# A gather moved, a third block's rows transposed inside its arm, and the last expert's block in two copies

## The chip, the core and the metric

The kernel runs on one core of one Trainium2 chip. The metric is the time of one execution on the device in microseconds (us). The program is timed in several executions, and the median counts.

The core has five engines, each with its own instruction queue: TensorE (PE, with its weight loads as PEld), VectorE (DVE), ScalarE (ACT), GpSimd (POOL) and SyncE (SP, which here issues most DMA transfers). They meet through semaphores.

## What is computed

Three layers one after the other: windowed attention, a soft mixture of experts, and a mixture in which each token goes to one expert or to none. The change touches the last one alone:

```python
def _moe2_ref(x, w_skip, w_gate, w1, w2):
    N, D = x.shape                      # 1152 tokens, 512
    E = w_gate.shape[1]                 # 8 experts, hidden width 1024
    do_compute = x @ w_skip > 0
    out = x.copy()
    xc = x[do_compute]
    logits = xc @ w_gate
    e_idx = np.argmax(logits, axis=1)
    logits_s = logits - logits.max(-1, keepdims=True)
    probs = np.exp(logits_s)
    probs /= probs.sum(-1, keepdims=True) + 1e-09
    gate_w = probs[np.arange(len(xc)), e_idx]
    y = np.zeros_like(xc)
    for e in range(E):
        mask = e_idx == e
        h = np.maximum(xc[mask] @ w1[e], 0.0)
        y[mask] = gate_w[mask, None] * (h @ w2[e])
    out[do_compute] = xc + y
    return out
```

With the inputs that are timed, experts 0 to 7 get 116, 207, 129, 66, 298, 17, 114 and 51 tokens.

## The kernel before

**Arithmetic.** All matrix products run on TensorE in a 32-bit format on operands that are split into a high and a low part; the products high x high, high x low and low x high are added up in PSUM. So weights and rows each pass a split: ACT copies the high part (L347 for weights, L896 for rows, `xs`), VectorE subtracts it from the original (L351, L898). The tiles of weights are `wa1h`, `wa1l`, `wa2h`, `wa2l` and the same with `wb`: two sets that the experts use in turn, the digit for the first or second layer.

**Blocks.** The last stage, from about 486 us on, handles each expert's tokens in blocks of 128 rows. POOL gathers a block's rows from memory with an indirect DMA (`gather`, L869, into `xg`, or `xj` for a third block), by indices that the routing has computed (`idg`). `xpose` turns them on TensorE in four transposes of 128x128 (`tr4`, L379), and `xsplit` makes high and low parts. `block(e, j, ...)` is the two layers for block `j` of expert `e`: matmuls at L920, ACT at L944 and L965, VectorE at L968, and at the end VectorE scales by the gate and adds (L1004). POOL's `scatter` (L877) writes the rows to the output. A block with at most 64 rows has a small form in which the high and low parts of 64 rows share one pass of 128 columns.

**Branches.** The first block of each expert always runs (for expert 7, in one of the two forms). What an expert has beyond 128 tokens runs inside `tails(e)`, a branch at L1126: `more` runs the second block in one of two arms, full or small (`rows`, L1081), and a third block inside another branch (L1116). For experts 6 and 7 there is one `tails(6)`, placed ahead of expert 7's first block: inside it lie the tails of both and `deep()`, which serves experts with more than 384 tokens and loads weights again. It is entered if any of these has work (`nv[2] > 0`). Here experts 1, 2 and 4 enter the branch (2 for one row), 4 also its third block, with 42 rows; for experts 0, 3, 5 and for 6 with 7 the branch is jumped. `hint(e)` announces the branch's outcome on PE, ACT, DVE and POOL some way ahead of it, not on SP.

**Order.** The program is written by a planner: `add(engine, cost, function, rd, wr, new, prio)` registers an operation, and `plan.run()` issues all that is registered, engine by engine, by list scheduling with the costs and priorities given. Each engine then works through its queue in that order. Expert 0's block is in one plan with the two layers ahead of it. In it the routing's tables are still being made for the second half of their columns: VectorE's `wy` (L755) feeds the `tab` matmuls on TensorE (L760), from which `gates` and `ids` are worked out, which the end of the block needs.

Of the kernel before, what the change touches and what calls it, by code (L numbers as in the profile page):

```python
# [13 lines left out]
ALU = mybir.AluOpType  # L14
# [9 lines left out]
E2 = 8  # L24
TT = NT // 128
XP, XE, XF = -0.5, 0, 2
# [9 lines left out]
def f32(ap):  # L36
    return ap.bitcast(F32)
# [70 lines left out]
class Plan:  # L108
# [6 lines left out]
    def add(self, eng, dur, fn, rd=(), wr=(), prio=0.0, new=None, slack=0.0):  # L115

        o = Op()
        o.slack = slack
        o.eng, o.dur, o.fn, o.prio, o.seq, o.acq = eng, dur, fn, prio, len(self.ops), list(new or ())
        wr = list(wr) + o.acq  # L120
        deps = set()
        for x in rd:
            if x in self.w:
                deps.add(self.w[x])
        for x in wr:
            if x in self.w:
# [96 lines left out]
def fused_kernel(ctx: ExitStack, tc: tile.TileContext, q, k, v, dp, w1, w2, wskip, wgate, m1, m2, out):  # L223
    nc = tc.nc
    PE, ACT, DVE, POOL, SP = nc.tensor, nc.scalar, nc.vector, nc.gpsimd, nc.sync
# [19 lines left out]
    ident = const.tile([128, 128], F32, name="ident")  # L245
# [36 lines left out]
    add = plan.add  # L282
# [600 lines left out]
    def xpose(b, pr, after=[]):  # L883
        p = pt_r.buf()
        add("PE", 0.44, lambda: tr4(p.tile, b.tile), rd=[b, "ident"] + after, new=[p], prio=pr)
        return xsplit([p], pr)

    def xsplit(ps, pr):

        x, w = M["xs"].buf(), KC // len(ps)  # L890
        for i, p in enumerate(ps):
            ks = range(i * w, (i + 1) * w)
            v = lambda p=p: (p.tile if p.ring is pt_r else p.tile.rearrange("p (a n) -> p a n", a=4))[:, 0:w]
            hi = lambda i=i: x[:, i * w:(i + 1) * w, :, 0]
            lo = lambda i=i: x[:, i * w:(i + 1) * w, :, 1]
            add("ACT", c_act(128 * w), lambda v=v, hi=hi: ACT.copy(out=hi(), in_=v()), rd=[p, "M"] + ([x] if i else []),  # L896
                wr=[(x, "h", k) for k in ks], new=None if i else [x], prio=pr)
            add("DVE", c_dve(128 * w), lambda v=v, hi=hi, lo=lo: DVE.tensor_tensor(out=lo(), in0=v(), in1=f32(hi()), op=ALU.subtract),  # L898
                rd=[p, x] + [(x, "h", k) for k in ks], wr=[(x, "l", k) for k in ks], prio=pr)
            p.close()  # L900
        return x
# [123 lines left out]
    with tc.manual_schedule():  # L1025
# [33 lines left out]
        add("X", 0.0, open_moe2, rd=["pf"], wr=["M"] + [("x2", t) for t in range(TT)] + [(x, f) for x in ("hh", "hl") for f in range(FC)], slack=-0.43)  # L1059
        xgs, xts = {}, {}  # L1060
        for j in range(2):
            xgs[0, j] = gather(0, j, 0.0 if j else 2.0)
        w_pass("r", 1, 1)
        w_pass("r", 1, 2)
        xts[0, 0] = xsplit(first, -5)
# [7 lines left out]
        def over(e, i):  # L1073

            return (nv[0] & (7 * 8 ** e)) > (i - 1) * 8 ** e

        def rows(e, j, x, xt):

            state = ([(b, b.left, b.closed, b.slot) for b in (x, xt)],
                     [(r, len(r.free), None if r.slots is None else list(r.slots)) for r in Ring.made])  # L1080
            with tc.If(over(e, 2 * j + 1), preferred_fallthrough_block=False if e == E2 - 1 and j == 0 else None) as c:  # L1081
                block(e, j, x, xt)
                if j == 0:
                    ahead(e)
                scatter(e, j, x)
                plan.run()
            with c.Else():
                for b, left, closed, slot in state[0]:
                    b.left, b.closed, b.slot = left, closed, slot
                for r, n, slots in state[1]:  # L1090
                    r.free, r.slots = [0.0] * n, slots
                block(e, j, x, xt, small=True)
                if j == 0:
                    ahead(e)
                scatter(e, j, x, 64)
                plan.run()

        def further(e):

            return nv[2] > 0 if e == E2 - 2 else over(e, 2)  # L1100

        def hint(e):

# [10 lines left out]
        def more(e, xt):  # L1114
            for j in (1, 2):
                with tc.If(over(e, 4)) if j == 2 else ExitStack():  # L1116
                    if j == 2 and e >= E2 - 2:
                        xgs[e, j] = gather(e, j)
                    if j == 2 or xt is None:
                        xt = xpose(xgs[e, j], 0)  # L1120
                        plan.run()
                    rows(e, j, xgs[e, j], xt)

        def tails(e, xt):

            with tc.If(further(e), label=f"more{e}", preferred_fallthrough_block=True):  # L1126
                if e < E2 - 2:
                    more(e, xt)
                else:
                    with tc.If(over(e, 2)):  # L1130
                        more(e, xt)
                    with tc.If(over(e + 1, 2)):
                        more(e + 1, None)
                    with tc.If(nv[1] > 0):
                        deep()

        def deep():

            for e in range(E2):
                n = nc.values_load(R["cnt"][0:1, e:e + 1], min_val=0, max_val=NT,  # L1140
                                   skip_runtime_bounds_check_because="counts of at most all tokens")
                with tc.If(n > 384):
                    w_pass("r", e, 1)
                    w_pass("r", e, 2)
                    plan.run()
                    with ExitStack() as levels:
                        for j in range(3, TT):
                            if j > 3:
                                levels.enter_context(tc.If(n > 128 * j))
                            x = gather(e, j)  # L1150
                            block(e, j, x, xpose(x, 0))
                            scatter(e, j, x)
                            plan.run()
            w_pass("r", E2 - 1, 1)
            w_pass("r", E2 - 1, 2)
            plan.run()

        for e in range(E2):
            last = e == E2 - 1
            if e < E2 - 2:  # L1160
                xgs[e, 2] = gather(e, 2, 7, [("g2", 0)])
            if last:
                plan.run()
                rows(e, 0, xgs[e, 0], xts[e, 0])
                continue
            block(e, 0, xgs[e, 0], xts[e, 0], amid=None if e else route_gates)
            if e == 0:
                add("X", 0.0, counts, rd=["cnt"], wr=["nv"], slack=1.5)
            ahead(e)
            xts[e, 1] = xpose(xgs[e, 1], XP, [("g2", XE if e else 3)])  # L1170
            xts[e, 1].pin = e == E2 - 2
            if e:
                w_pass("r", e + 1, 1)
                w_pass("r", e + 1, 2)
            for d in range(1 if e == 0 else 2, 3):
                for j in range(2):
                    if e + d < E2:
                        xgs[e + d, j] = gather(e + d, j, 0 if e else 2 * d + j - 1 + (d == 1 and j), [("g10", 0)] if e else [])
            xts[e + 1, 0] = xpose(xgs[e + 1, 0], XP, [("g2", XF if e else 3)])
            scatter(e, 0, xgs[e, 0])  # L1180
            plan.run(**(OFF if e else dict(SP=1.75, PE=1.4, ACT=2.1, POOL=0.6, DVE=0.6)))
            if e == 0:
                route_ps.close()
                M["mmx"].pool = ctx.enter_context(tc.tile_pool(name="ps_x", bufs=3, space=PSUM))
            tails(e, xts[e, 1])


# [26 lines left out]
```

## Time and profile before

| | us |
|---|---|
| runs shown | 655.6, 651.71, 649.83; median 651.71 |
| the profiled execution | 652.86 |
| its span, first to last instruction | 651.1 |
| PE busy | 627.8 (96%) |
| DVE busy | 315.3 (48%) |
| ACT busy | 234.2 (36%) |
| POOL busy | 70.8 (11%) |

Times in the rows are microseconds from the start of the span. A row of the timeline is one instruction, or several alike in a row (x4): start, duration, engine, line, operation, tiles, shapes; in brackets stands how long the engine had been idle before and what ended that. Matmuls overlap each other, so their spacing says more than the duration. Queue names with a q (POOLq, DVEq) are the instructions of an engine's sequencer: branches, semaphores, drains. The granted clock (PEclk) of a stretch is a share of TensorE's full speed, 2.4 GHz; its other level is 1.2 GHz.

### The profile page before, as it was taken

The numbers are of one execution on the slowest core, as the hardware profiler recorded it, in microseconds if no ns is written. First come the engines' busy times: TensorE is split into PE (matmuls) and PEld (weight loads), VectorE is DVE, ScalarE is ACT, GpSimd is POOL, SyncE is SP. The second block draws the span as 40 slices with busy tenths as digits, with TensorE's granted clock in tenths as the row PEclk, the third lists the DMA queues.
The fourth block names the chain that finished last, engine by engine and source line by source line (L and its number), as shares of the span: only waits on it lengthen the run. The fifth ranks groups of instructions, "written<-read, shape, count | busy, mean of one in ns | idle before, by whom it ended". The sixth has DMA issues, their size and how long they took to land. (4 is left out here: it accounts for less than half of the span.)

```text
span 651.1 us, 9941 instructions
## 1 busy us (share of the span) xinstructions
PE 627.8 (96%) x3794; PEld 550.1 (85%) x3794; DVE 315.3 (48%) x685; ACT 234.2 (36%) x488; POOL 70.8 (11%) x103
## 2 busy tenths in 40 slices
PE   8899999999999999999999999999998999999976
PEld 6688898898989898989898998989896878787865
DVE  5897631127412124512124425436478855871871
ACT  5678630025301013401113311202524644853751
POOL 4123320000000000000000000000004321420310
PEclk9999999999999999999999999999998999999998
DMA  9992100006500004400002502010547967791630
GB/s 225 214 294 65 34 2 1 1 1 209 179 1 1 1 1 129 130 1 0 1 1 97 163 15 82 2 66 32 173 164 281 312 227 260 213 385 62 209 127 9
DMA packets 55688, 71.13 MB, mean 109 GB/s; under 512 B 32921, under 2 KB 32921, under 8 KB 55616
## 3 DMA queue, kind: packets, MB, share of 16 engines
q1 hardware_dynamic: 52912, 62.17, 30.4%
q0 software_dynamic: 2704, 8.02, 4.0%
q8 instruction: 42, 0.69, 0.4%
q14 instruction: 30, 0.25, 0.1%
HBM read 63.48 MB, written 7.47 MB: 109 GB/s over the span
## 5 line engine op out<-in xcount | busy, mean ns | idle before, releaser
L540 PE MATMUL mm<-xth,wa1h 128*128 128x384 f32 (+1 forms) x416 | 137.1, 330 | 0.0
L540 PE MATMUL mm<-xtl,wa1h 128*128 128x384 f32 (+1 forms) x416 | 135.3, 325 | 0.2 <-DVE xtl L489 0.2
L540 PE MATMUL mm<-xth,wa1l 128*128 128x384 f32 (+1 forms) x416 | 135.2, 325 | 0.0
L546 ACT ACTIVATE hh<-mm 128x384 fp32r<-128x384 f32 (+1 forms) x104 | 48.4, 466 | 234.7 <-PE mm L540 229.7
L561 PE MATMUL mm<-wa2h,hh 128*128 128x512 f32 (+1 forms) x296 | 117.0, 395 | 0.0
L548 DVE SCALAR_TENSOR_TENSOR hl<-mm,hh 128x384 fp32r<-128x384 f32 (+1 forms) x104 | 54.6, 526 | 126.2 <-ACT hh L546 125.7
L561 PE MATMUL mm<-wa2h,hl 128*128 128x512 f32 (+1 forms) x296 | 115.1, 389 | 0.0
L561 PE MATMUL mm<-wa2l,hh 128*128 128x512 f32 (+1 forms) x296 | 115.0, 389 | 0.0
L540 PEld LDWEIGHTS mm<-xth,wa1h 128*128 128x128 f32 x416 | 78.3, 188 | 0.7 <-issue 0.2
L540 PEld LDWEIGHTS mm<-xtl,wa1h 128*128 128x128 f32 x416 | 78.3, 188 | 0.8 <-DVE xtl L489 0.4
L540 PEld LDWEIGHTS mm<-xth,wa1l 128*128 128x128 f32 x416 | 78.3, 188 | 0.0
L561 PEld LDWEIGHTS mm<-wa2h,hl 128*128 128x128 f32 x296 | 55.7, 188 | 12.4
L561 PEld LDWEIGHTS mm<-wa2h,hh 128*128 128x128 f32 x296 | 55.8, 188 | 11.2
L561 PEld LDWEIGHTS mm<-wa2l,hh 128*128 128x128 f32 x296 | 55.9, 189 | 11.0
L573 DVE SCALAR_TENSOR_TENSOR x<-mm,prob,x 128x512 f32<-128x512 f32 (+1 forms) x28 | 20.5, 732 | 92.0 <-PE mm L561 91.2
L347 ACT CAST wa2h<-raw 128x1024 fp32r<-128x1024 f32 x32 | 33.4, 1050 | 25.6 <-PE mm L561 18.6
L351 DVE TENSOR_TENSOR wa2l<-raw,wa2h 128x1024 fp32r<-128x1024 f32 x32 | 39.0, 1229 | 5.5 <-ACT wa2h L347 5.5
L784 POOL DMA_INDIRECT x<-scr,id x1 | 1.3, 1254 | 364.5 <-DVE id L801 364.5
L351 DVE TENSOR_TENSOR wa1l<-raw,wa1h 128x1024 fp32r<-128x1024 f32 x32 | 38.1, 1224 | 2.4 <-ACT wa1h L347 2.4
L347 ACT CAST wa1h<-raw 128x1024 fp32r<-128x1024 f32 x32 | 32.0, 1048 | 17.9 <-DMA raw<-in_moe_w_dram 9.7
L968 DVE SCALAR_TENSOR_TENSOR ht<-pt,ht 128x512 fp32r<-128x512 f32 (+2 forms) x27 | 15.1, 568 | 33.1 <-ACT ht L965 30.8
L877 POOL DMA_INDIRECT out_dram<-xg,ids x11 | 16.0, 1458 | 83.1 <-DVE xg L1004 64.4
(202 smaller groups left out, 881.4 us busy)
## 6 DMA issues: line engine op xcount, KB each, us to landing
raw<-in_moe_w_dram SPq DMA_DIRECT2D x96, 512.0 KB
scr<-x SPq DMA_DIRECT2D x9, 256.0 KB
out_dram<-x SPq DMA_DIRECT2D x9, 256.0 KB
qn<-in_q_dram SPq DMA_DIRECT2D x8, 256.0 KB
kn<-in_k_dram SPq DMA_DIRECT2D x8, 256.0 KB
vn<-in_v_dram SPq DMA_DIRECT2D x8, 256.0 KB
qn<-in_q_dram SPq DMA_DIRECT2D x2, 128.0 KB
kn<-in_k_dram SPq DMA_DIRECT2D x2, 128.0 KB
```

The costliest lines, as they stand in the source:

```text
L347: (POOL.tensor_copy if hpool else DVE.tensor_copy if hdve else ACT.copy)(out=aps()[0], in_=b.tile)
L351: (POOL if pool else DVE).tensor_tensor(out=l, in0=b.tile, in1=f32(h), op=ALU.subtract)
L540: PE.matmul(out=ps[:, 0:n], lhsT=wa[a][:, kk, f * 128:(f + 1) * 128], rhs=x[:, kk, g0:g0 + n], start=(i == 0), stop=(i == 3 * KC - 1))
L546: add("ACT", c_act(n), lambda: ACT.activation(out=hh[:, f, 0:n], in_=ps[:, 0:n], func=ACTF.Relu), rd=[ps], wr=[("hh", f)], prio=-1)
L548: add("DVE", c_dve(n), lambda: DVE.scalar_tensor_tensor(out=hl[:, f, 0:n], in0=ps[:, 0:n], scalar=0.0, in1=f32(hh[:, f, 0:n]), op0=ALU.max ...
L561: PE.matmul(out=ps[:, 0:c1 - c0], lhsT=x[:, f, o:o + 128], rhs=wa[a][:, f, c0:c1], start=(f == 0 and i == 0), stop=(f == FC - 1 and i == 2))
L573: DVE.scalar_tensor_tensor(out=z, in0=y, scalar=prob[:, t, e:e + 1], in1=z, op0=ALU.mult, op1=ALU.add)
L784: add("POOL", 1.0, lambda: POOL.indirect_dma_start(out=R["x0"], out_offset=None, in_=scr[0:128 * (GT + 1), :], in_offset=bass.IndirectOffs ...
L877: add("POOL", 1.0, lambda: POOL.indirect_dma_start(out=out, out_offset=bass.IndirectOffsetOnAxis(ap=R["ids"][0:n, j, e:e + 1], axis=0), in ...
L968: add("DVE", c_dve(w * n), lambda: DVE.scalar_tensor_tensor(out=ht[:, s, n:2 * n], in0=p[:, 0:w, 0:n], scalar=0.0, in1=f32(ht[:, s, 0:n]), ...
```

## The change

1. **Expert 0.** `xts[0, 1]`, the transposed rows of its second block, is no longer made ahead of `tails(0)`; it is made inside the arm if that runs. The gather (0, 1) gets priority 2.5 in place of 0.0, and so goes behind (1, 0) and (0, 0).
2. **Blocks that were not transposed ahead**, third blocks above all, are transposed inside their arm by `xpair`, in two pieces of two transposes each, over 128 rows in the full arm and 64 in the small one, in place of one `xpose` of 128 rows ahead of the branch on the block's size. `xsplit` gets a width `n` for that.
3. **Experts 6 and 7.** `tails(6)` is gone. `last()` tests `nv[2] == 0`: if so, expert 7's block runs (`rows`, first copy); in the other arm come the tails of 6 and 7, `deep()`, and `rows` a second time. The hint is turned round with it. `keep` and `back` save and restore the planner's state of buffers between the two copies.

```diff
+    def xpair(b, n):
+        ps = [pt_r.buf() for _ in range(2)]
+        for i, p in enumerate(ps):
+            def tr(i=i, p=p):
+                for g in range(2):
+                    PE.transpose(out=p[:, g, 0:n], in_=b[0:n, 256 * i + 128 * g:256 * i + 128 * g + 128],
+                                 identity=ident[0:n, 0:n])
+
+            add("PE", 0.22, tr, rd=[b, "ident"], new=[p], prio=0)
+        return xsplit(ps, 0, n)
+
-    def xsplit(ps, pr):
+    def xsplit(ps, pr, n=128):
...
-            xgs[0, j] = gather(0, j, 0.0 if j else 2.0)
+            xgs[0, j] = gather(0, j, 2.5 if j else 2.0)
...
-                block(e, j, x, xt)
+                block(e, j, x, xt or xpair(x, 128))
...
-                block(e, j, x, xt, small=True)
+                block(e, j, x, xt or xpair(x, 64), small=True)
...
-            return nv[2] > 0 if e == E2 - 2 else over(e, 2)
+            return nv[2] == 0 if e == E2 - 2 else over(e, 2)
...
-                    if j == 2 or xt is None:
-                        xt = xpose(xgs[e, j], 0)
                         plan.run()
-                    rows(e, j, xgs[e, j], xt)
+                    rows(e, j, xgs[e, j], xt if j == 1 else None)
...
             with tc.If(further(e), label=f"more{e}", preferred_fallthrough_block=True):
-                if e < E2 - 2:
-                    more(e, xt)
-                else:
-                    with tc.If(over(e, 2)):
-                        more(e, xt)
-                    with tc.If(over(e + 1, 2)):
-                        more(e + 1, None)
-                    with tc.If(nv[1] > 0):
-                        deep()
+                more(e, xt)
+
+        def last(xt):
+
+            e = E2 - 1
+            mine = e, 0, xgs[e, 0], xts[e, 0]
+            state = keep(*mine[2:])
+            with tc.If(nv[2] == 0, label=f"more{e - 1}", preferred_fallthrough_block=True) as c:
+                rows(*mine)
+            with c.Else():
+                back(state)
+                with tc.If(over(e - 1, 2)):
+                    more(e - 1, xt)
+                with tc.If(over(e, 2)):
+                    more(e, None)
+                with tc.If(nv[1] > 0):
+                    deep()
+                rows(*mine)
...
-                rows(e, 0, xgs[e, 0], xts[e, 0])
+                last(xts[e - 1, 1])
...
-            xts[e, 1] = xpose(xgs[e, 1], XP, [("g2", XE if e else 3)])
-            xts[e, 1].pin = e == E2 - 2
+            if e:
+                xts[e, 1] = xpose(xgs[e, 1], XP, [("g2", XE)])
+                xts[e, 1].pin = e == E2 - 2
...
-            tails(e, xts[e, 1])
+            if e < E2 - 2:
+                tails(e, xts.get((e, 1)))
```

## Rows read from the trace of the kernel before

**Rows 1.** The page, busy us (share of the span) and instructions of each engine
```profile
PE 627.8 (96%) x3794; PEld 550.1 (85%) x3794; DVE 315.3 (48%) x685; ACT 234.2 (36%) x488; POOL 70.8 (11%) x103
```

**Rows 2.** Windows: length, busy PE, PEld, DVE, ACT, POOL; PEclk, DMA share, GB/s
```profile
505.00:531.00 26.00, 25.03 (x120) 20.30 (x119) 16.93 (x20) 14.28 (x20) 6.55 (x6) 1.00 0.82 285
```

**Rows 3.** Timeline, expert 0's first block
```profile
497.08 0.60 PE L379 MATMUL pt<-ident,xg 128*128 128x128 f32 x4
...
498.72 0.67 DVE L755 TENSOR_TENSOR wy<-w,oj 128x216 bf16<-128x216 bf16 x2
...
500.03 0.73 PE L379 MATMUL pt<-ident,xg 128*128 128x128 f32 x4 [2.35 <-DMA xg<-scr,idg]
...
500.80 0.78 PE L920 MATMUL mm<-wb2h,ht 128*128 128x512 f32 x1
...
504.44 0.48 PE L920 MATMUL mm<-wa1h,xs 128*128 128x512 f32 x1 [0.15 <-PEq L1126]
```

**Rows 4.** Windows around three stops of TensorE
```profile
500.00:504.50 4.50, 4.32 (x15) 3.27 (x15) 4.06 (x10) 0.65 (x1) 1.12 (x1) 0.62 1.02 384
592.00:594.40 2.40, 0.88 (x7) 0.56 (x5) 1.44 (x2) 0.61 (x1) 0.92 (x1) 1.00 0.00 0
...
634.00:637.00 3.00, 3.00 (x7) 2.42 (x8) 0.00 (x0) 0.00 (x0) 0.00 (x0) 0.51 0.08 27
```

**Rows 5.** Timeline, last eight matmuls of expert 3's block and what follows
```profile
564.78 0.40 PE L920 MATMUL mm<-wa2h,ht 128*128 128x512 f32 x1
...
566.97 0.49 PE L920 MATMUL mm<-wb1h,xs 128*128 128x512 f32 x1
```

**Rows 6.** Timeline, expert 4's third block
```profile
592.45 0.75 DVE L1004 SCALAR_TENSOR_TENSOR xg<-mmx,gates,xg 128x512 f32<-128x512 f32 x1 [3.27 <-PE mmx L920]
592.88 0.61 ACT L896 CAST xs<-pt 128x512 fp32r<-128x512 f32 x1 [4.42 <-PE pt L379]
...
593.53 0.69 DVE L898 TENSOR_TENSOR xs<-pt,xs 128x512 fp32r<-128x512 f32 x1 [0.33 <-ACT xs L896]
...
594.36 0.47 PE L920 MATMUL mmx<-wb1h,xs 128*128 128x512 f32 x1 [1.52 <-DVE xs L898]
...
596.30 0.28 PE L920 MATMUL mmx<-wb1h,xs 128*128 128x256 f32 x1
...
601.14 0.28 ACT L965 ACTIVATE ht<-pt 128x128 fp32r<-128x128 f32 x1 [0.87 <-PE pt L959]
...
601.45 0.29 DVE L968 SCALAR_TENSOR_TENSOR ht<-pt,ht 128x128 fp32r<-128x128 f32 x1 [2.01 <-ACT ht L965]
```

**Rows 7.** Timeline, the start of expert 7's block
```profile
630.84 0.47 PE L920 MATMUL mm<-wa1h,xs 128*128 128x512 f32 x1 [0.68 <-PEq L1126]
...
633.99 0.80 PE L920 MATMUL mm<-wa1l,xs 128*128 128x512 f32 x1 [2.67 <-DVEq L1126]
...
637.07 0.28 PE L920 MATMUL mm<-wa1h,xs 128*128 128x256 f32 x1
```

**Rows 8.** Line L1126, 617 to 636: count, ns min/median/max, first and last start
```profile
L1126 SPq EVENT_SEMAPHORE  x9: 17/17/17, 624.4 to 625.7; - x9
...
L1126 DVEq EVENT_SEMAPHORE  x3: 21/21/21, 618.8 to 634.0; - x3
...
L1126 POOLq INC_SWDGE_SEM  x2: 829/841/853, 618.0 to 634.8; - x2
...
L1126 SPq COMPARE_BRANCH  x1: 45/45/45, 619.3 to 619.3; - x1
...
L1126 DVEq COMPARE_BRANCH  x1: 74/74/74, 630.2 to 630.2; - x1
```

**Rows 9.** The end: timeline, then line L1209 on POOL and SP
```profile
646.19 0.91 POOL L877 DMA_INDIRECT out_dram<-xg,ids  x1 [13.22 <-DVE xg L1004]
...
L1209 POOLq DRAIN  x3: 44/115/4094, 646.1 to 650.8; - x3
...
L1209 SPq EVENT_SEMAPHORE  x13: 17/28/13112, 635.6 to 651.0; - x13
```

More of the change, by code (lines that the diff above doesn't have):

```diff
@@ L892, in xsplit @@
             ks = range(i * w, (i + 1) * w)
[L893 to L896, printed above, removed]
+            v = lambda p=p: (p.tile if p.ring is pt_r else p.tile.rearrange("p (a n) -> p a n", a=4))[:, 0:w, 0:n]
+            hi = lambda i=i: x[:, i * w:(i + 1) * w, 0:n, 0]
+            lo = lambda i=i: x[:, i * w:(i + 1) * w, 0:n, 1]
+            add("ACT", c_act(n * w), lambda v=v, hi=hi: ACT.copy(out=hi(), in_=v()), rd=[p, "M"] + ([x] if i else []),
                 wr=[(x, "h", k) for k in ks], new=None if i else [x], prio=pr)
-            add("DVE", c_dve(128 * w), lambda v=v, hi=hi, lo=lo: DVE.tensor_tensor(out=lo(), in0=v(), in1=f32(hi()), op=ALU.subtract),
+            add("DVE", c_dve(n * w), lambda v=v, hi=hi, lo=lo: DVE.tensor_tensor(out=lo(), in0=v(), in1=f32(hi()), op=ALU.subtract),
                 rd=[p, x] + [(x, "h", k) for k in ks], wr=[(x, "l", k) for k in ks], prio=pr)
@@ L1075, in over, with keep, back @@
             return (nv[0] & (7 * 8 ** e)) > (i - 1) * 8 ** e
+        def keep(*bufs):
+            return ([(b, b.left, b.closed, b.slot) for b in bufs],
+                    [(r, len(r.free), None if r.slots is None else list(r.slots)) for r in Ring.made])
+        def back(state):
+            for b, left, closed, slot in state[0]:
+                b.left, b.closed, b.slot = left, closed, slot
+            for r, n, slots in state[1]:
+                r.free, r.slots = [0.0] * n, None if slots is None else list(slots)
         def rows(e, j, x, xt):
-            state = ([(b, b.left, b.closed, b.slot) for b in (x, xt)],
-                     [(r, len(r.free), None if r.slots is None else list(r.slots)) for r in Ring.made])
+            state = keep(x, *([xt] if xt else []))
             with tc.If(over(e, 2 * j + 1), preferred_fallthrough_block=False if e == E2 - 1 and j == 0 else None) as c:
-                block(e, j, x, xt)
+                block(e, j, x, xt or xpair(x, 128))
                 if j == 0:
@@ L1087, in rows @@
             with c.Else():
[L1088 to L1091, printed above, removed]
-                block(e, j, x, xt, small=True)
+                back(state)
+                block(e, j, x, xt or xpair(x, 64), small=True)
                 if j == 0:
@@ L1118, in more @@
                         xgs[e, j] = gather(e, j)
-                    if j == 2 or xt is None:
-                        xt = xpose(xgs[e, j], 0)
                         plan.run()
-                    rows(e, j, xgs[e, j], xt)
+                    rows(e, j, xgs[e, j], xt if j == 1 else None)
         def tails(e, xt):
             with tc.If(further(e), label=f"more{e}", preferred_fallthrough_block=True):
-                if e < E2 - 2:
-                    more(e, xt)
-                else:
-                    with tc.If(over(e, 2)):
-                        more(e, xt)
-                    with tc.If(over(e + 1, 2)):
-                        more(e + 1, None)
-                    with tc.If(nv[1] > 0):
-                        deep()
+                more(e, xt)
[6 more added lines that the diff above has]
+            with c.Else():
+                back(state)
+                with tc.If(over(e - 1, 2)):
[5 more added lines that the diff above has]
+                rows(*mine)
         def deep():
@@ L1158, in fused_kernel @@
         for e in range(E2):
-            last = e == E2 - 1
             if e < E2 - 2:
                 xgs[e, 2] = gather(e, 2, 7, [("g2", 0)])
-            if last:
+            if e == E2 - 1:
                 plan.run()
-                rows(e, 0, xgs[e, 0], xts[e, 0])
+                last(xts[e - 1, 1])
                 continue
```

## The prediction

> **What bounds the kernel now.** I read the page first. TensorE is busy for 96% of the span [rows 1], so a change pays only where TensorE stands still or runs slowly, and the edits touch only the last stage, from 486 us on. I therefore read that stage in windows and then its timeline, looking for idle time in front of matmuls. In most stretches there is next to none: 25.03 of 26.00 us are busy between 505 and 531 [rows 2]. Three places stand out, and they are the three that the diff touches.
>
> First, in expert 0's first block, TensorE stops for 2.35 us in front of the second set of row transposes, until a gather lands at 500.03 [rows 3]. Behind that stop the granted clock is 0.62 on average over 500.0 to 504.5 [rows 4], a mix of the levels 2.4 and 1.2 GHz, and the last eight matmuls and the boundary take 3.64 us (500.80 to 504.44 [rows 3]), where the same in expert 3 takes 2.19 (564.78 to 566.97 [rows 5]).
>
> Second, ahead of expert 4's third block it stops for 1.52 us, until VectorE has made the low halves of the rows [rows 6].
>
> Third, ahead of expert 7 it waits 0.68 us, runs one matmul, and waits 2.67 us for VectorE's queue at L1126 [rows 7]. Then the granted clock is 0.51 over 634 to 637 [rows 4], that is 1.2 GHz: seven matmuls take 3.08 us, from 633.99 to 637.07 [rows 7].
>
> The sum is made against the profiled execution, 652.86 us with a span of 651.1; it lies 1.15 us above the median of the runs shown. The two slow stretches explain a difference of that size if the clock falls in some executions only; without the stops the forecast should not depend on that.
>
> **Part 1: expert 0.** For the inputs here expert 0 has 116 tokens, so its second block never runs. Still its rows were gathered first and transposed in the main path. The change drops that transposition (four transposes at 497.08, 0.60 us [rows 3], an ACT cast of 0.61 us and a VectorE subtract of 0.69 us by the same shapes in [rows 6]) and moves the gather behind those for (1,0) and (0,0). Dropped casts cost nothing; the gather that moves later has no reader until expert 0's tail, which is jumped.
>
> The rows of expert 1 now come with the first gather. They have landed by 497.08, since the first gather's transposes started then. So the only set of transposes runs at 497.08 to 497.68. Next in TensorE's order are still the two `tab` matmuls, which need VectorE's `wy`, done at 498.72 + 0.67 = 499.39 [rows 3]. TensorE answers a VectorE result after about 0.14 us (593.53 + 0.69 to 594.36 [rows 6]); with the `tab` pair started, the eight left matmuls of the block begin at about 499.60 instead of 500.80. The stop shrinks to about 1.6 us. The nearest row is the 1.52 us stop ahead of expert 4's third block, in which the granted clock stayed 1.00 [rows 4] and behind which nine matmuls took 1.94 us [rows 6], 0.22 each, so at 2.4 GHz. So I take full clock and the 2.19 us of [rows 5] for the eight and the boundary. The next block starts at 499.60 + 2.19 = 501.79 instead of 504.44 [rows 3]: gain 2.6 us. If the clock falls all the same, they take the 3.64 us of before, and the gain is 1.2.
>
> Does the shift survive? Weights for the coming experts are cast by ACT and VectorE, and these are anchored on TensorE's progress by the order. Expert 1 runs a second block with no weights of its own, TensorE is 96% busy there, and ACT and VectorE are at 14.28 and 16.93 of 26.00 us [rows 2]. They have slack to move by 2.6 us. A gain of nothing here would need a weight load to be late, with DMA at 0.82 [rows 2]. This is the lower bound, and it lies in the range. The upper bound is a `wy` that comes early because VectorE loses its 0.69 us subtract: up to 0.7 us more.
>
> **Part 2: expert 4's third block.** The transposes move behind the branch and into the arm, in two pieces of two, 64 rows wide; VectorE then subtracts two pieces of 128 columns. Prices are those of the nearest shapes: 0.28 us for an ACT copy of 128x128 and 0.29 us for a VectorE operation of 128x128 [rows 6]. ACT's first copy starts no later than the old one at 592.88 and is done by 593.16. VectorE is busy with the last block's output, 592.45 to 593.20 [rows 6]; its first subtract ends at 593.49. With 0.14 us to TensorE the first matmul starts at 593.63 instead of 594.36: gain 0.7. The second piece ends at 593.78, in time for the fifth matmul, some 1.0 us behind the first by that spacing. Bounds: 1.0 if the branch costs nothing, 0.3 if VectorE's own jump into the small arm delays the subtract.
>
> **Part 3: expert 6 to 7.** Before, every engine jumps at L1126 over the tails of 6 and 7 and over `deep()`, and expert 7's block stands behind the join. VectorE's branch stands at 630.2 and its next semaphore operation at 634.0 [rows 8], 3.8 us. `deep()` may rewrite expert 7's weights, so block 7 cannot trust the weights until VectorE has passed the join. That is the 2.67 us wait [rows 7]. After the change the usual case falls through into its own copy of the block, inside which nothing rewrites weights, so this wait has no cause. What is late next is the first matmul itself, 630.84, whose 0.68 us of queue work at the boundary I keep (bound: 0.5 us of it goes). From there at full clock the first nine matmuls of a small block take 594.36 to 596.30, 1.94 us [rows 6]. So the ninth starts at 632.78 instead of 637.07 [rows 7]: gain 4.3, bounds 4.3 to 4.8.
>
> The cost: the far jump now comes at the end, since the fall-through copy must jump over the other one, and this jump carries no hint. By [rows 8] a far jump takes 3.8 us on VectorE and 5.1 us on SP (619.3 to 624.4), whose branch has no hint. What hides it is the last scatter: it is issued at 646.19, and Pool's drain runs 4.09 us from 646.1 while the rows land at 635.6 + 13.11 = 648.7 [rows 9]. I take it as hidden; 5.1 us would show 1.0 of itself.
>
> The Trainium skill, in "Runtime: NRT & Kernel Launch", section "Instruction fetch mechanics", says that a taken branch to a target outside the two pages at hand must fetch the target by DMA before it goes on. The 3.8 us agree, and this rule speaks against the new end jump, which is rival 2. The skill's "Advanced Engine Details and Errata", section "Control Flow Timing", puts a compare-and-branch at about 108 ns; by that the end jump would cost nothing and the sum would stand, but the rows of this far jump are some thirty times longer.
>
> **Sum.** 2.6 + 0.7 + 4.3 = 7.6 off 652.86 gives 645.3. Its own range is 644.3 to 646.9 (tails 0.5 and 0.3 better; 1.0 of end jump and 0.4 to 0.6 of parts 1 and 2 worse).
>
> **Rivals.**
> Rival 1, the clock falls in expert 0 all the same. For: 1.6 us of idle is a little more than the 1.52 that did no harm, and the work ahead differs. Against: that row is near. Gain there 1.2, time 646.7.
>
> Rival 2, the end jump surfaces. For: 5.1 us on SP without a hint, and a drain that might start its 4.09 us only behind the jump. Against: a drain that waits for the landing would not start anew, and the two other Pool drains, with nothing in flight, take 0.04 and 0.12 us [rows 9]. Time 646.3 (5.1 alongside the drain) to 650.4 (5.1 in front of it).
>
> Rival 3, part 3 does not do what it says: VectorE's wait stays in the new arm, since the join of the branch ahead can make a wait too. Only parts 1 and 2 count: 652.86 − 3.3 = 649.6.
>
> Rival 4, the other side: everything at the end in series. Pool levels its semaphores behind the landing (two increments of 0.84 us [rows 8]), then jumps 5.1, then drains 4.09, then some 0.9 of barrier: 2.5 + 1.7 + 5.1 + 4.1 + 0.9 = 14.3 us behind the scatter's issue instead of 4.9 (646.19 to 651.1). That is 9.4 more, 1.8 above the gains: 654.7. It decides once the series costs more than 7.6. Against: today Pool's drain overlaps the landing [rows 9].
>
> **How the numbers follow.** Forecast 0.55, rival 1 0.15, rival 2 0.15, rival 3 0.11, rival 4 0.04. The low end 643.4 has the forecast with all upper bounds at once (0.7 + 0.3 + 0.5) and some room; the high end 649.2 takes in rival 1 and the half of rival 2 up to there and leaves out rivals 3, 4 and a third of rival 2, 0.20 in all. About 1% is what a measurement of this kernel can tell from no change: 6.5 us, or 645.2. The saving of 7.6 is just over that of the profiled execution, the time just short of it against the median; I count 0.7 of the forecast's chance and 0.3 of rival 1's as faster, 0.43; slower is rival 4, 0.04; the rest, 0.53, is within.
>
> **What would show it.** Part 1: one set of L379 transposes near 497, eight matmuls at 0.23 us spacing behind 499.6, granted clock 1.00 over 500 to 502. Part 2: two pieces of VectorE subtract of about 0.29 us, and a stop of about 0.8 us ahead of the third block. Part 3: no wait on VectorE's queue in front of block 7, and the clock full behind it; at the end a jump between the last scatter and the drain. It is wrong if the stop ahead of block 7 keeps over 2 us, if the time from the last scatter to the end grows beyond 6 us, or if a weight cast becomes late behind expert 0.

## The result: slower by 1%, and where the time went

The changed kernel takes 659.98 us (median; 658.09 to 661.92), the kernel before 651.28 in the same comparison. The ratio is 1.0106, with a 95% interval of 1.0075 to 1.0138. So it is slower by about 1%, and 645.3 was forecast. The profiled execution has a span of 656.3 us against 651.1.

I read TensorE's first matmul of each block in both profiles. Where the stage begins differs by some tenths of a microsecond up to 2.4 us between executions, but here by 0.13 alone, so the starts can be set against each other. First the timeline of TensorE after, the columns as in the rows ahead of the prediction:

```profile
499.01 0.55 PE L760 MATMUL tab<-wy,r 128*128 128x216 bf16 x2 [1.47 <-DVE w L747]
499.33 0.48 PE L931 MATMUL mm<-wb2h,ht 128*128 128x512 f32 x1
...
501.56 0.48 PE L931 MATMUL mm<-wa1h,xs 128*128 128x512 f32 x1 [0.15 <-PE mm L931]
...
506.42 0.63 PE L972 MATMUL pt<-ident,hr 128*128 128x128 f32 x4 [0.91 <-DVEq L1141]
...
529.83 0.51 PE L931 MATMUL mm<-wb1h,xs 128*128 128x512 f32 x1 [1.94 <-PEq L1133]
...
554.36 0.51 PE L931 MATMUL mm<-wa1h,xs 128*128 128x512 f32 x1 [0.50 <-PEq L1133]
...
572.51 0.77 PE L931 MATMUL mm<-wb1h,xs 128*128 128x512 f32 x1 [4.94 <-PEq L1141]
...
577.27 0.97 PE L931 MATMUL mm<-wb1h,xs 128*128 128x512 f32 x3 [1.30 <-DVE wa1l L351]
...
601.66 0.50 PE L931 MATMUL mmx<-wb1h,xs 128*128 128x512 f32 x1 [0.65 <-DVE xs L909]
...
637.32 0.40 PE L931 MATMUL mm<-wa1h,xs 128*128 128x512 f32 x1
...
639.18 0.28 PE L931 MATMUL mm<-wa1h,xs 128*128 128x256 f32 x1
```

And two starts of the kernel before that stood in no group:

```profile
530.70 0.51 PE L920 MATMUL mm<-wb1h,xs 128*128 128x512 f32 x1 [0.97 <-PEq L1116]
...
553.61 0.50 PE L920 MATMUL mm<-wa1h,xs 128*128 128x512 f32 x1 [0.43 <-PEq L1116]
```

| TensorE starts | before | after | lead of the changed kernel |
|---|---|---|---|
| expert 1's block | 504.44 [rows 3] | 501.56 | 2.88 |
| expert 2's block | 530.70 | 529.83 | 0.87 |
| expert 3's block | 553.61 | 554.36 | -0.75 |
| expert 4's block | 566.97 [rows 5] | 572.51 | -5.54 |
| expert 4's third block | 594.36 [rows 6] | 601.66 | -7.30 |
| expert 7's block | 630.84 [rows 7] | 637.32 | -6.48 |
| its ninth matmul | 637.07 [rows 7] | 639.18 | -2.11 |
| end of the span | 651.1 | 656.3 | -5.2 |

Read from top to bottom, the three gains are all there: 2.9 us at expert 0, 0.9 at the third block (the stop is 0.65 instead of 1.52), and 5.2 at expert 7, where the lag falls from 7.30 to 2.11 (no stop ahead of the block, none behind its first matmul, and full clock). Four things take them back:

- 2.0 us between expert 1 and expert 2: a new stop of 0.91 us, and 1.94 instead of 0.97 ahead of expert 2.
- 1.6 us in expert 2, and 1.3 us in expert 4, where the granted clock fell behind the stops.
- 4.8 us ahead of expert 4, a stop of 4.94 us on TensorE's own queue, and 1.30 us for a late weight cast behind it.
- 3.1 us at the end.

The clock, by windows of the changed kernel (columns as in [rows 2]): 0.68 and 0.52, where the kernel before had 1.00 in the same places. The length of the stop alone does not decide this: in two runs below (part 1 alone, and the one with 116 idle instructions) the clock stayed at 1.00 behind stops of 1.94 and 2.29 us ahead of expert 2.

```profile
529.80:533.50 3.70, 3.67 (x11) 3.01 (x12) 2.90 (x3) 2.67 (x3) 2.50 (x3) 0.68 0.38 79
572.50:575.60 3.10, 3.09 (x8) 2.47 (x8) 2.03 (x2) 2.94 (x3) 1.10 (x2) 0.52 0.83 288
```

**The stops on TensorE's own queue.** They are jumps. The branch instructions of TensorE's sequencer behind expert 1 (L1133) and behind expert 3 (L1141), with count, duration in ns (min/median/max) and start; first the changed kernel, then the one before (L1116, L1126):

```profile
L1133 PEldq COMPARE_BRANCH  x2: 190/2246/4302, 525.0 to 529.6; - x2
...
L1141 PEldq COMPARE_BRANCH  x1: 8087/8087/8087, 564.3 to 564.3; - x1
...
L1116 PEldq COMPARE_BRANCH  x2: 228/258/288, 526.8 to 530.4; - x2
...
L1126 PEldq COMPARE_BRANCH  x1: 353/353/353, 563.5 to 563.5; - x1
```

The branch behind expert 3 took 8.09 us, in the kernel before 0.35; that behind expert 1 took 4.30, before 0.23. Matmuls that were already handed on still run meanwhile, so the stops are shorter than the branches. What TensorE waits for is visible in the view of the DMA queues: instructions come over a queue of their own, 16 KB a piece (queue q8; the page has 41 packets and 0.67 MB). They are TensorE's: between 93.4 and 459.5 us of the kernel before, 15 such packets start while TensorE runs 1918 matmuls and 1917 weight loads, 256 instructions to a packet.

```profile
93.40:459.60 366.20, 366.20 (x1918) 331.26 (x1917) 127.03 (x309) 76.69 (x136) 1.25 (x1) 1.00 0.15 50
...
q8 instruction: 15, 0.25, 0.3%
```

Before, from the hint to the jump behind expert 3 (554.0 to 563.5), one such piece comes:

```profile
q1 hardware_dynamic: 355, 1.32, 38.4%
q0 software_dynamic: 129, 0.27, 13.8%
q8 instruction: 1, 0.02, 0.8%
```

After, in 555 to 568, none; the next comes in 568.0 to 572.6, while weight loads keep the DMA engines busy (q1, 90.9%), and then TensorE goes on at 572.5:

```profile
q1 hardware_dynamic: 600, 2.13, 44.1%
q0 software_dynamic: 275, 0.77, 29.9%
q14 instruction: 1, 0.01, 0.2%
...
q1 hardware_dynamic: 785, 1.54, 90.9%
q0 software_dynamic: 13, 0.02, 6.9%
q8 instruction: 1, 0.02, 1.3%
```

So the code at the jump's target was not there, and it had to be fetched behind the weights. The packets' own times bear this out in all profiles: each of TensorE's branches that took over 1 us ended 1.4 to 1.6 us after such a packet had landed. Where the packet was still to come, it started 0.4 to 1.0 us after the branch where the DMA share was under 0.2 (ahead of expert 7 and at the end), and 1.2 to 5.7 us after it where the share was 0.9 or more (behind experts 1, 3 and 5). This is what the Trainium skill says in "Runtime: NRT & Kernel Launch", section "Instruction fetch mechanics": instructions come in blocks of 16 KiB, 256 of them, one after the other, and a taken branch out of the two blocks at hand waits for a fetch. The trace agrees with 4.3 and 8.1 us. Why these two jumps, which both kernels have, became long is what the experiments had to find.

**The end.** Pool's last scatter, and Pool's drains:

```profile
648.34 0.91 POOL L877 DMA_INDIRECT out_dram<-xg,ids  x1 [8.06 <-POOLq L1149]
...
L1234 POOLq DRAIN  x3: 46/109/3006, 652.4 to 656.0; - x3
```

From the scatter to the end it is 8.0 us, before 4.9 (646.19 to 651.1 [rows 9]). The long drain started 0.1 us ahead of the scatter's issue before [rows 9]; now it starts at 652.4, behind the far jump (Pool's branch stands at 649.4), and still takes 3.0 us, though the last packet of the scatter's queue (q0) had ended at 651.0.

### The profile page after: what moved, and what is told of

Its sections match the earlier page's. It is cut to its first block, busy times and chain, and to the rows that moved or that the text cites. A ratio compares the mean times of both kernels' runs of the same rounds, so it can differ in the third digit from the quotient of the medians.

```text
span 656.3 us, 9927 instructions
## 1 busy us (share of the span) xinstructions
PE 626.9 (96%) x3790; PEld 549.4 (84%) x3790; DVE 314.0 (48%) x685; ACT 233.3 (36%) x488; POOL 75.7 (12%) x103
## 5 line engine op out<-in xcount | busy, mean ns | idle before, releaser
L931 PE MATMUL mm<-wb1h,xs 128*128 128x512 f32 x64 | 23.9, 445 | 8.8 <-PEq L1141 4.9
```

The lines of the kernel that those rows point to most:

```text
L931: PE.matmul(out=ps[:, 0:cols.stop - cols.start], lhsT=op(k), rhs=ring[f"{c}{a}"][:, k, cols], start=(n == 0 and k == ks[0] and a == "h"), ...
```

## The experiments

The first theory: **places**. The change alters how many instructions lie between jumps and their targets, even in arms that never run; so branch, hint and target fall differently into the pieces of 256 instructions, and a jump whose target is in no piece at hand waits. The rival: **timing**. Part 1 brings TensorE to the branches 2 us earlier, and the fetches come too late for that.

Where idle instructions are added below, they stand in a body that is jumped with these inputs, so they only shift places.

### Places moved, nothing else

The kernel before gets 19 idle transposes, 38 instructions; the changed kernel 90, 180 instructions.

```diff
         def more(e, xt):
+            if e == 0:
+                u = pt_r.buf()
+                add("PE", 0.0, lambda: [PE.transpose(out=u[:, 0, :], in_=ident, identity=ident)
+                                        for _ in range(19)], rd=["ident"], new=[u])
+                u.close()
```

> The kernel before, with 19 idle transposes (38 TensorE instructions) put into expert 0's second-block body, which is jumped with these inputs. Nothing that executes changes; only the places of TensorE's later instructions move by 38. Theory of places (the two long jumps behind experts 1 and 3 of the changed kernel come from where branch and target stand in TensorE's program): the jumps behind experts 1 and 3 take 4 to 8 us here too, TensorE stands still for about 2 us more and about 5 us more, and the time is 5 to 9 us above the kernel before (ratio 1.008 to 1.014). Theory of timing (they come from TensorE reaching the branches about 2 us earlier): no change, ratio within 0.997 to 1.003, and both jumps stay at 0.2 to 0.4 us.

Measured: 660.44 us, ratio 1.0105 (1.0075 to 1.0134). The kernel before, with nothing else than 38 instructions that never run, is as slow as the changed kernel (though by another sum: it has neither the three gains nor the longer end). Both jumps are long (behind expert 1, L1120, and behind expert 3, L1130):

```profile
L1120 PEldq COMPARE_BRANCH  x2: 190/1976/3762, 526.6 to 530.6; - x2
...
L1130 PEldq COMPARE_BRANCH  x1: 4585/4585/4585, 563.7 to 563.7; - x1
```

The stops are not cut like those of the changed kernel: 1.49 us ahead of expert 4, and another of 3.19 us after nine of its matmuls, which again ends 1.3 us after a packet of instructions has landed (572.7, to 574.0).

> The changed kernel, with 90 idle transposes (180 TensorE instructions) in the same jumped body. Theory of places: at these places the jump behind expert 1 has its target in a part that was loaded long before, and the hint ahead of expert 3's jump loads its target again, so the stops of 1.94 and 4.94 us ahead of experts 2 and 4 shrink to under 1.0 and about 0.2, the clock stays full behind them, and the time is 8 to 11 us under that of the changed kernel, 649 to 652 (0.997 to 1.001 of the kernel before). Theory of timing: still 658 to 662, ratio 1.01.

Measured: 647.85 us, ratio 0.9915 (0.9882 to 0.9947), against 1.0106 without the idle instructions; better than expected by 1 us or more. The jump behind expert 3 takes 0.37 us, and the stop ahead of expert 2 is 0.44 us:

```profile
L1145 PEldq COMPARE_BRANCH  x1: 365/365/365, 563.1 to 563.1; - x1
...
530.23 0.51 PE L931 MATMUL mm<-wb1h,xs 128*128 128x512 f32 x1 [0.44 <-PEq L1137]
```

Both runs speak for places: in the first nothing is added but instructions that never run, in the second TensorE comes to these branches no later than in the changed kernel. Timing is not quite out by them alone, since the first run's profile reaches the branch behind expert 1 some 1.1 us earlier than the kernel before, counted from the stage's first matmul; the next run decides that.

### Each part alone

Part 2's new instructions all lie in arms that don't run, except for expert 4. Part 1 moves four transposes from the main path into a jumped body, so that behind it everything stands where it stood. Each kernel takes the lines of its part from the diff above and leaves the rest as it was. Part 1:

```diff
-            xgs[0, j] = gather(0, j, 0.0 if j else 2.0)
+            xgs[0, j] = gather(0, j, 2.5 if j else 2.0)
...
-            xts[e, 1] = xpose(xgs[e, 1], XP, [("g2", XE if e else 3)])
-            xts[e, 1].pin = e == E2 - 2
+            if e:
+                xts[e, 1] = xpose(xgs[e, 1], XP, [("g2", XE)])
+                xts[e, 1].pin = e == E2 - 2
...
-            tails(e, xts[e, 1])
+            tails(e, xts.get((e, 1)))
```

> Part 1 alone (gather order, no transposition of expert 0's second block ahead of the branch). The four transposes move into the jumped body, so TensorE's instructions from expert 1 on stand where they stood before. Theory of places: the clock stays full in expert 0, the next block starts 2.6 to 2.9 us earlier, some of it is lost again to a later stop of about 0.9 us in expert 1's block, no jump gets long, and the time is 1.5 to 2.5 us under the kernel before (ratio 0.996 to 0.998). Theory of timing: the two long jumps appear as in the changed kernel, ratio 1.005 to 1.012.

Measured: 653.17 us, ratio 1.0001 (0.9975 to 1.0026). The jumps behind experts 1 and 3 are not long, as the theory of places says. This rules timing out: counted from the stage's first matmul, these two branches come after 39.4 and 77.0 us here and are short, and with the 38 instructions they came after 40.0 and 77.1 us and were long. But the expected gain of 0.3% is not there either. It is lost ahead of expert 2:

```profile
530.80 0.51 PE L920 MATMUL mm<-wb1h,xs 128*128 128x512 f32 x1 [1.94 <-ACT wa1h L347]
...
L1116 PEldq COMPARE_BRANCH  x2: 228/258/287, 526.0 to 530.5; - x2
...
L1116 PEldq EVENT_SEMAPHORE  x1: 51/51/51, 528.9 to 528.9; - x1
```

The view puts the stop down to ACT, but TensorE's sequencer says more: it was at the join at 528.9, and its next instruction came at 530.5. In the kernel before these two are 529.8 and 530.4. TensorE arrives 0.9 us earlier and goes on at the same time. In both a piece of instructions has landed by 529.0 (here one q8 packet in 527.5 to 529.1), and TensorE goes on 1.5 to 1.6 us after it, as behind the long jumps. So the kernel before has this wait too, and what part 1 gains flows into it: the stop of 1.94 us stands here without a long jump. With the 180 instructions above, which put this jump elsewhere, the stop is 0.44 and the gain stays; this accounts for a part of what that run had beyond the expectation.

Part 3:

```diff
-            return nv[2] > 0 if e == E2 - 2 else over(e, 2)
+            return nv[2] == 0 if e == E2 - 2 else over(e, 2)
...
-                rows(e, 0, xgs[e, 0], xts[e, 0])
+                last(xts[e - 1, 1])
```

> Part 3 alone (expert 7's block in two copies). TensorE's instructions up to expert 6 stand where they stood before. Both theories: no long jump behind experts 1 and 3; the wait on VectorE ahead of block 7 is gone and the clock full behind it (gain 4.3 to 4.9 us), and the far jump stands between the last scatter and the drain (loss 2.5 to 3.5 us): in sum 1 to 2.4 us under the kernel before, ratio 0.996 to 0.9985. If the end jump is hidden by the drain: 4.3 to 4.9 under, ratio 0.993.

Measured: 651.54 us, ratio 0.9974 (0.995 to 0.9998), as expected. TensorE runs from expert 6 into expert 7 without a gap, and the end is longer:

```profile
629.38 1.07 PE L931 MATMUL mm<-wb2h,ht 128*128 128x512 f32 x4
630.29 0.40 PE L931 MATMUL mm<-wa1h,xs 128*128 128x512 f32 x1
...
632.15 0.28 PE L931 MATMUL mm<-wa1h,xs 128*128 128x256 f32 x1
...
641.31 0.91 POOL L877 DMA_INDIRECT out_dram<-xg,ids  x1 [8.06 <-POOLq L1151]
...
L1235 POOLq DRAIN  x3: 46/109/3005, 645.8 to 649.4; - x3
```

The group of expert 6 in the kernel before:

```profile
629.09 1.07 PE L920 MATMUL mm<-wb2h,ht 128*128 128x512 f32 x4
```

The ninth matmul comes 2.77 us behind the last group of expert 6 (632.15 - 629.38), before 7.98 (637.07 - 629.09): 5.2 us gained. From the scatter to the end of the span (649.7) it is 8.4 us, 3.5 more.

Part 2:

```diff
-                block(e, j, x, xt)
+                block(e, j, x, xt or xpair(x, 128))
...
-                block(e, j, x, xt, small=True)
+                block(e, j, x, xt or xpair(x, 64), small=True)
...
-                    if j == 2 or xt is None:
-                        xt = xpose(xgs[e, j], 0)
                         plan.run()
-                    rows(e, j, xgs[e, j], xt)
+                    rows(e, j, xgs[e, j], xt if j == 1 else None)
```

> Part 2 alone. Of what executes it shortens only the stop ahead of expert 4's third block (1.52 to 0.65 us in the changed kernel). But it makes each expert's jumped body 8 TensorE instructions longer, so that from expert 3 on the jump starts 24 or more places later than before. Theory of places: that alone brings the long jump behind expert 3 (4 to 8 us) and the longer stop ahead of expert 2: 4 to 9 us above the kernel before, ratio 1.006 to 1.014. If the long jumps come from part 1 or 3, or need parts 1 and 2 together: 0.5 to 0.9 us under the kernel before, ratio 0.997 to 1.001.

Measured: 658.26 us, ratio 1.0072 (1.0048 to 1.0096). This is the part that makes the kernel slow, and not by what it executes:

```profile
L1135 PEldq COMPARE_BRANCH  x1: 7761/7761/7761, 563.6 to 563.6; - x1
...
571.54 0.77 PE L931 MATMUL mm<-wb1h,xs 128*128 128x512 f32 x1 [4.61 <-PEq L1135]
```

It makes both arms of each third block longer by four transposes in place of one set ahead of them: 8 instructions for each expert, 24 ahead of the jump behind expert 3 (34 in the changed kernel, where expert 0's second block is transposed in both its arms too). The jump behind expert 1 is long here as well (3.64 us), but the stop ahead of expert 2 is only 1.21 us, before 0.97: that jump costs little by itself.

Parts 1 and 3 together, the changed kernel with the lines of part 2 taken back:

> Parts 1 and 3 without part 2: TensorE's instructions of experts 1 to 6 stand where they stood before. Theory of places: no long jump behind expert 3; the stop ahead of expert 2 is as long as with part 1 alone (1.9 us, which takes most of part 1's gain), the end jump costs 3 us: between part 1 and part 3 alone, 0.994 to 0.999 of the kernel before. If parts 1 and 3 brought the long jumps: ratio above 1.005.

Measured: 652.03 us, ratio 0.9968 (0.9946 to 0.999). Without part 2 neither of the two jumps is long; the stop ahead of expert 2 is 1.70 us, and the longer end stays. So the long jumps need part 2, and parts 1 and 3 don't bring them.

### The two long jumps apart

The changed kernel gets 58 idle transposes in the third-block body of expert 2, the kernel before 46.

```diff
         def more(e, xt):
             for j in (1, 2):
                 with tc.If(over(e, 4)) if j == 2 else ExitStack():
+                    if e == 2 and j == 2:
+                        u = pt_r.buf()
+                        add("PE", 0.0, lambda: [PE.transpose(out=u[:, 0, :], in_=ident, identity=ident)
+                                                for _ in range(58)], rd=["ident"], new=[u])
+                        u.close()
```

> The changed kernel with 116 idle TensorE instructions in the third-block body of expert 2, which is not run: places move from expert 3 on alone. Theory of places: the stop of about 1.9 us ahead of expert 2 stays as in the changed kernel, that of 4.9 us ahead of expert 4 goes (0.2 us), with the late weight cast behind it: 5 to 8 us under the changed kernel, ratio to the kernel before 0.996 to 1.002. If one cause sat behind both (a stop at expert 2 delays a load that expert 4 waits for): the stop ahead of expert 4 stays and the ratio is 1.01.

Measured: 652.46 us, ratio 0.9993 (0.9975 to 1.0011). With the place of expert 3's jump alone moved, the stop ahead of expert 4 is 0.15 us and 7.5 us of the changed kernel's 660 are gone, though the stop ahead of expert 2 stays (2.29 us) and a new one of 1.77 us comes ahead of expert 3, behind the body that the idle instructions made longer. So the jump behind expert 3, with the lower clock and the late cast that follow it, is the larger part of the loss.

> The kernel before with 92 idle TensorE instructions in the third-block body of expert 2, which is not run. Counted in pieces of 256 instructions, the jumps behind experts 3 and 5 then start one piece behind their hint and land two pieces further on. Theory that a hint only works from the branch's own piece: both jumps get long (3 to 8 us in place of 0.35), 5 to 14 us above the kernel before, ratio 1.007 to 1.02. Theory that a hint is only left out where the target lies in the piece after the branch's: both stay at 0.35, ratio 0.998 to 1.002.

Measured: 658.86 us, ratio 1.0073 (1.0049 to 1.0098). Both hinted jumps are long, though their targets lie two pieces further on, as in the kernel before:

```profile
L1130 PEldq COMPARE_BRANCH  x1: 3685/3685/3685, 568.4 to 568.4; - x1
...
L1130 PEldq COMPARE_BRANCH  x1: 6487/6487/6487, 618.6 to 618.6; - x1
```

What is common to the long ones: a boundary between pieces lies between the hint and the branch. I counted TensorE's instructions in the compiled programs, in units of 256, with 36 more for what stands ahead of them. This offset is not measured but chosen to fit; any value from 27 to 42 divides the jumps below in the same way.

| the jump behind expert 3 | hint | branch | target | jump, us |
|---|---|---|---|---|
| before; parts 1, 3, 1 and 3 | 31.48 | 31.94 | 33.82 | 0.35 |
| changed | 31.61 | 32.07 | 33.98 | 8.09 |
| part 2 | 31.57 | 32.04 | 33.94 | 7.76 |
| before + 38 | 31.63 | 32.09 | 33.97 | 4.59 |
| before + 92 | 31.84 | 32.30 | 34.18 | 3.69 |
| changed + 116 | 32.07 | 32.53 | 34.43 | 0.34 |
| changed + 180 | 32.32 | 32.78 | 34.69 | 0.37 |

Over all profiles here, counted the same way, 31 hinted jumps with hint and branch in one piece took 0.34 to 0.49 us. Of 12 with a boundary between, 8 took 3.1 to 8.1 us and 4 took 0.34 to 0.46. So the division is a fit to these jumps; one run alone was made to test it, that with the 92 instructions, and there it came out as forecast. Three of those four have the branch a third of a piece or more behind the boundary, the fourth 0.12. It may be that the target is asked for only when the branch's piece is entered, and that the lead and the load on the DMA engines then decide; that reading is not tested, and the fourth speaks against it. That the far jump ahead of expert 7 took 3.07 us in the kernel before in spite of its hint fits as well (hint 38.73, branch 39.19): with 92 instructions more, and both in one piece, it took 0.35.

### The end, and a version that is faster

```diff
-            with tc.If(nv[2] == 0, label=f"more{e - 1}", preferred_fallthrough_block=True) as c:
-                rows(*mine)
-            with c.Else():
-                back(state)
+            with tc.If(nv[2] > 0, label=f"more{e - 1}", preferred_fallthrough_block=True) as c:
                 with tc.If(over(e - 1, 2)):
                     more(e - 1, xt)
...
                 rows(*mine)
+            with c.Else():
+                back(state)
+                rows(*mine)
```

(The hint is turned back with it.)

> Part 3 alone with its arms exchanged: the rare tails and the second copy of block 7 come first, the usual copy of block 7 last, so that the usual case takes the far jump ahead of block 7 and runs out into the end of the program. If a copy of its own is what removed the wait on VectorE, and the far jump costs only where nothing covers it: the jumps ahead of block 7 (3 to 4 us on VectorE, Pool and ACT) lie under matmuls, no wait on VectorE's queue ahead of block 7, no jump between the last scatter and the drain; 4.3 to 5.5 us under the kernel before, ratio 0.992 to 0.9935, some 3 us better than part 3 as made. If the place ahead of the block is what makes the wait (the arm that is jumped to must wait for VectorE's jump): the stop of 2 to 3 us is back and the ratio is 0.998 to 1.001.

Measured: 648.15 us, ratio 0.9945 (0.9919 to 0.9972); a little less gain than expected. The far jump ahead of expert 7 (3.25 us on TensorE) now lies under matmuls, a stop of 0.29 us is left, and no wait on VectorE's queue appears:

```profile
630.33 0.47 PE L931 MATMUL mm<-wa1h,xs 128*128 128x512 f32 x1 [0.29 <-DVE wa2l L351]
...
641.40 0.91 POOL L877 DMA_INDIRECT out_dram<-xg,ids  x1 [8.56 <-POOLq L1151]
```

From the scatter to the end (646.4) it is 5.0 us, as before the change. So it is the copy that removed the wait on VectorE, and the far jump costs where nothing covers it. That the wait came from `deep()` and the weights, as the prediction has it, was not tested apart from that.

> The changed kernel with its last arms exchanged in the same way and with the 180 idle instructions in expert 0's jumped body: all three gains, none of the three losses. From the run with the 180 instructions (647.85 where before had 653.02) less the 3 us of the end jump: 644 to 646, ratio 0.986 to 0.989. If the exchange brings the wait on VectorE back: 0.991 to 0.994.

Measured: 646.22 us (645.37 to 646.9), ratio 0.9887 (0.9857 to 0.9917). This beats both kernels: the three parts, expert 7's arms exchanged, and 180 instructions that never run, to keep the jumps at good places. The time is just above the 644 to 646 that were expected. In it the stops that the prediction spoke of are gone or near their predicted size, and the time is the one that was predicted for the change, within 1 us; that it comes so near is in part luck, as shown below.

```profile
508.97 0.63 PE L972 MATMUL pt<-ident,hr 128*128 128x128 f32 x4 [0.91 <-DVEq L1145]
530.88 0.51 PE L931 MATMUL mm<-wb1h,xs 128*128 128x512 f32 x1 [0.44 <-PEq L1137]
553.80 0.51 PE L931 MATMUL mm<-wa1h,xs 128*128 128x512 f32 x1 [0.43 <-PEq L1137]
...
L1238 POOLq DRAIN  x3: 46/109/2954, 641.2 to 644.7; - x3
```

## Why the prediction was wrong, step by step

**The step that failed.** The sum costs only what executes: it has no term for jumps and boundaries that the edits merely move to other places, and so put their change at nothing. Measured, the places alone are worth about 12.5 us (1.0106 against 0.9915 of 653 us, the changed kernel without and with 180 idle instructions). The second term at nothing was the end jump; it shows 3.1 us. Two of the signs that the prediction named for being wrong did come: over 6 us from the last scatter to the end, and a late weight cast (1.30 us, in expert 4).

**Part 1, expert 0: right in place, wrong in reach.** One set of transposes, eight matmuls from 499.33 (499.60 was worked out), full clock, the next block at 501.56 (501.79). The clock did not fall behind a stop of 1.47 us, here and in the five other profiles with part 1, so rival 1 is out. But in the profile of part 2 alone the clock stayed full behind a stop of 2.04 us too; so the 1.4 us that the sum counts for the clock are not lost in every execution without the change. What failed here is "does the shift survive?". It looked for late weights on ACT, VectorE and DMA. The lead was lost to a stop of 0.91 us in expert 1's block, on VectorE's queue (its far jump over expert 0's tail runs from 503.3 to 506.3, before from 504.4 to 507.4), and then at the join behind expert 1, where TensorE waits for its own instructions. The 0.97 us in front of expert 2 stood in the trace of before and was not asked about, since TensorE was 96% busy there [rows 2].

**Part 2, third block: right in size (0.87 us for 0.7), and the loss of the whole.** Only its executed instructions were costed. It also makes arms longer that never run, and this moved branch and target of every later jump. Run alone it costs 0.7%. The prediction named the Trainium skill's rule on taken branches and applied it to the far jump at the end alone. The missing step was to ask of each jump that the code moves whether its target is still at hand.

**Part 3, expert 7: right.** The wait on VectorE is gone and the clock is full; 5.2 us came of the 4.3 to 4.8, mainly since the 0.68 us that I kept at the boundary went too.

**The end: wrong.** The far jump was taken as hidden under the drain. The drain starts only behind the jump and takes about 3 us, also when the scatter has landed before it starts. This is rival 2 in its second form, with 3.1 us for the 5.1 that was priced. The argument against it, that the two other drains are short, did not hold for the first drain behind a scatter.

**The rivals.** Rivals 1, 3 and 4 did not come: full clock at expert 0, no wait on VectorE, and no series of 14 us at the end (it is 8.0). The result lies on rival 4's side for a reason that none of the five cases had. With the two losses taken away the kernel gains 6.6 us by the medians (652.77 to 646.22) and 7.4 by the ratio (1 - 0.9887 of 652.77), where 7.6 was forecast. The terms differ more than their sum: in the profile of that run, counted from the stage's first matmul, TensorE leads the kernel before by 2.2 us at expert 2 (2.6 forecast), by 1.2 more at the third block (0.7) and by 5.2 more at expert 7's ninth matmul (4.3), while the stage itself began 2.4 us later in that execution. Two slips in the working changed nothing: 1.94 us from the first to the ninth matmul are eight steps of 0.24, not nine of 0.22, and 645.3 less 0.5 and 0.3 is 644.5, not 644.3.

## What to carry to other kernels

In a kernel whose program is longer than what an engine holds, each edit that changes the length of code ahead of a jump changes other jumps too, and code that is never run counts; so compare the branch instructions of both profiles (their durations, on the engine's own queue) before looking for the cause in the edit itself. Have a few idle instructions in a body that is never run at hand, as a test for it, and as a remedy until the next edit moves the code again. A far jump belongs where another engine's work covers it: ahead of the last block it left a stop of 0.29 us, behind the last scatter it cost 3 us.

## What the runs showed of the hardware that I had not expected

- 38 instructions that never run made the kernel 1.05% slower (1.0075 to 1.0134), and 180 made the changed one faster, from 1.0106 to 0.9915 of the kernel before.
- By a count with a fitted offset, all 31 hinted jumps with the hint in the branch's own piece of 256 instructions were short (0.34 to 0.49 us), and 4 of 12 where a boundary lies between. Why those four is open.
- Instructions come over the same DMA engines as the weights. Where the piece with its target was still to be fetched, a jump took TensorE 3.1 to 8.1 us, and it ended 1.4 to 1.6 us after a 16 KB packet had landed.
- The first drain of Pool behind a scatter takes about 3 us (2.95, 3.01 and 3.01 in three profiles; 4.09 before the change, where it starts with the scatter), even when it starts 4 us behind the scatter and 1.5 us after the scatter's last packet.
